# Moving the stores of x's first Fourier stage to GpSimd's queue, and cutting the last output stores another way

## The chip, the cores and the metric

The kernel runs on one core of one Trainium2 chip. The metric is the time of one execution on the device, in microseconds (us). The core has TensorE (PE, matrix products; PEld is its loading of weights), VectorE (DVE), ScalarE (ACT), GpSimd (POOL) and SyncE (SP). SP, ACT and POOL can issue DMA transfers, each in the order of its own instructions; the transfers of all three run on the same 16 DMA engines. In the profile, queue q1 is SP's, q10 ACT's and q0 GpSimd's, whose transfers are described by software on that engine.

## The reference

`u` has 2048 tokens of 448 channels. A layer norm, then the sum of the input, a state-space convolution over the tokens and a gated unit:

```python
def _A_ref(u, log_A_real, A_imag, C_real, C_imag, log_dt, D_skip):
    dt = jnp.exp(log_dt)
    A = -jnp.exp(log_A_real) + 1j * A_imag            # 448 x 256
    C = (C_real + 1j * C_imag) * dt[:, None]
    P = jnp.exp((A * dt[:, None])[:, :, None] * pos[None, None, :])
    K = 2.0 * jnp.einsum("dn,dnl->dl", C, P).real     # 448 x 2048
    y = irfft(rfft(u_t, 2 * L) * rfft(K, 2 * L), 2 * L)[:, :, :L]
    return y + u * D_skip                             # y back in token order

def _B_ref(x, w_gate, w_up, w_down):                  # 448 -> 1792 -> 448
    h = sigmoid(x @ w_gate) * (x @ w_up)
    return h @ w_down

xn = layernorm(u)
return u + _A_ref(xn, ...) + _B_ref(xn, ...)
```

## The kernel before, in words

Tokens stand in 16 blocks of 128 partitions. Two Python generators are interleaved: `glu()` is the gated unit, `conv()` the convolution. They write the program in one order, and the framework then orders each engine's instructions by a simulated timeline of its own (`schedule_with_timeline_sim=True`), within their dependences and a few explicit `issue_after` and priority marks. So an edit of one issue can move other rows.

`glu()` goes over the tokens in two halves of 8 blocks, and in each half over five groups of weight columns. For a group it makes the gate and up products (L709, tile `gu`), on ACT `th` (L717) and `hh` (L725), on DVE `hf` (L720) and `hl` (L727), then the down products (L825, tile `po`), which DVE adds to `acc` (L830). Numbers are carried as a high and a low part (`hh`, `hl`; `dh`, `dl`; `xh`, `xl`); `dl` is made on POOL (L786).

`conv()` first prepares coefficients and, for blocks 0 to 7, takes the first stage of x's Fourier transform: `x_spec` multiplies two normed blocks with a small table (L280), ACT copies the products into one of three buffers `x1a`, `x1b`, `x1c` (L293, L295) and stores them to `x1_d` in HBM, four stores for each pair of blocks. It is called four times, between 43 and 73 us. Then `kgen` makes the filter K in 56 chunks: POOL builds `me` and `mf` for two chunks at a time by repeated products (L508, L520; two buffers each), ACT squares part of `me` (L533) and makes the sines and cosines `S` (L548 to L551), DVE multiplies them into `Et` and `Ft` (L602 to L604), and PE sums over them (L616, tile `ko`).

At the end of the first half, still during `kgen`, blocks 8 to 15 are normed and transposed (`pair_norm`, `pair_turn`; L213, with the copies L219, L222, L225 on ACT and their low parts L220, L223, L226 on DVE), and `pair_first` takes their first Fourier stage: L280 again, four copies on ACT (L689), four stores on ACT's queue (L691). The copies land in tiles that share memory with `wraw` and `rd`, so the next pair's copies wait until the stores have landed. This happens four times, between 278 and 330 us.

After that, `spectra` multiplies the spectra and transforms back. The second half of `glu()` runs beside the rest of `kgen` and beside `spectra`. The function `out(src, b0, nb, ds, engs)` stores blocks `b0` to `b0+nb-1`, channels `ds`, as four DMAs, one for each 32 partitions, dealt to the queues `engs` in turn. `last(1, m)` adds the second half of the convolution's channels (L970) to all accumulators: `m` = 0, 2 to the blocks 0 to 7 (`ac`), `m` = 4, 6 to the blocks 8 to 15 (`accs[2]`, `accs[3]`). The variable `final` marks the last group of the second half: its t = 0 ends blocks 8 to 11, its t = 1 blocks 12 to 15.

Of the kernel before, what the change touches and what calls it, by code (L numbers as in the profile page):

```python
# [20 lines left out]
D = 448  # L21
# [18 lines left out]
H = D // 2  # L40
# [91 lines left out]
def s4d_glu_kernel(ctx, tc, io):  # L132
    nc = tc.nc
# [57 lines left out]
    def acc_tile():  # L191
        return pg.tile([128, 4, D], F32, name="acc", bufs=2)
# [37 lines left out]
    accs = [acc_tile() for _ in range(2)]  # L230

    def blocks(t, g, b0, nb):
        return t[g, :, b0 // 8, b0 // 4 % 2, b0 % 4 : b0 % 4 + nb]

    def out(src, b0, nb, ds, engs):

        for g in range(4):
            eng = engs[g % len(engs)]
            eng.dma_start(blocks(out_t, g, b0, nb)[:, :, ds], src[32 * g : 32 * g + 32, b0 % 4 : b0 % 4 + nb, ds])
# [33 lines left out]
    def row(b, g):  # L273
        return 32 * (b // 4 % 2) + 8 * g + 4 * (b // 8) + b % 4

    def x_first_stage(to, xn, g):

        s = slice(32 * g, 32 * g + 32)
        for i in range(2):
            nc.tensor.matmul(to[64 * i : 64 * i + 64], wx[s], xn[i][s], start=True, stop=True)  # L280

    def x_spec(xn, b0):

        x1s_ = []
        for _ in range(2):
            x1s_.append(slots[("x1a", "x1b", "x1c")[x1s[0] % 3]])
            x1s[0] += 1
        ps = psc[-1].tile([128, 2, 512], F32, name="tr", bufs=1)
        kk = [psc[-1].tile([128, 512], F32, name=n, bufs=1) for n in ("ko", "kp")]
        with tc.issue_after(glu_mm[0].ins):  # L290
            for j in range(4):
                x_first_stage((ps[:, j] if j < 2 else kk[j - 2])[:, :D], xn, j)
        nc.scalar.copy(x1s_[0], ps[:, :, :D])  # L293
        for j in range(2):
            nc.scalar.copy(x1s_[1][:, j], kk[j][:, :D])  # L295
        for p in range(2):
            r = row(b0, 2 * p)
            for h in range(2):
                to = x1_d[h].rearrange("(g r) k d -> g r k d", r=8)[r // 8 : r // 8 + 2, r % 8 : r % 8 + 2]
                nc.scalar.dma_start(to.rearrange("g i k d -> (i k) g d"), x1s_[p][:, :, H * h : H * h + H])  # L300
        yield 2 * WX

    def exp(ex, ki, fr, pl):
# [377 lines left out]
    def pair_first(b, xns):  # L681

        x1 = pg.tile([128, 2, D], F32, name="x1", tag="wraw", bufs=1)
        pss = [psg.tile([128, 512], F32, name="gu", bufs=4) for _ in range(4)]
        for g in range(4):
            x_first_stage(pss[g][:, :D], xns, g)
        for g in range(4):
            to = x1[:, g] if g < 2 else pg.tile([128, D], F32, name="x1", tag="rd", bufs=RB)
            nc.scalar.copy(to, pss[g][:, :D])  # L689
            r = row(b, g)  # L690
            nc.scalar.dma_start(  # L691
                x1_d[:, r : r + 2].rearrange("h i k d -> (i k) h d"), to.rearrange("p (h d) -> p h d", h=2)
            )

# [35 lines left out]
    def glu():  # L730
        for half in range(2):
# [4 lines left out]
            for fs_ in ORDER[half]:  # L736
# [3 lines left out]
                final = half == 1 and fs_ is ORDER[1][-1]  # L740
# [4 lines left out]
                if cross:  # L745
                    xts = {b: pair_load(b) for b in range(8, 16, 2)}
                    step = lambda f_, b: f_(b, xts[b])
                    mid = [(pair_norm, 8), None, (pair_first, 8), (pair_first, 10)]
                    end = [(), ((pair_turn, 8), (pair_norm, 10)), ((pair_turn, 10), (pair_norm, 12)), ((pair_turn, 12), (pair_norm, 14))]
                    downs = {(0, 0): (pair_first, 12), (0, 1): (pair_turn, 14), (0, 3): (pair_first, 14)}  # L750
# [54 lines left out]
                for t in range(2):  # L805
                    acc = accs[2 * half + t]
                    for b in range(4):
                        if final and (t, b) == (0, 1):

                            yield None  # L810
                        if final and t == 1 and b >= 2:

                            sp_mm[:] = glu_mm
                            for m in (4 * b - 8, 4 * b - 6):
                                lasts[0](1, m)
                            if b == 3:
                                out(accs[2], 8, 4, slice(H, D), (nc.sync, nc.scalar))
                                out(accs[3], 12, 3, slice(0, D), (nc.sync, nc.scalar))
                        po = psg.tile([128, D], F32, name="po", tag="gu", bufs=4)
                        bs = slice(128 * b, 128 * b + 128)  # L820
                        n = 0
                        with tc.issue_after(sp_mm[0].ins) if glu_on else nullcontext():
                            for (hh, hl), (dh, dl) in zip(hs[t], wts):
                                for a_, w_ in ((hh, dh), (hh, dl), (hl, dh)):
                                    glu_mm[:] = [nc.tensor.matmul(  # L825
                                        po, a_[:, bs], w_, start=(n == 0), stop=(n == 3 * fc - 1)
                                    )]
                                    n += 1
                        with hp(HP):
                            v.scalar_tensor_tensor(  # L830
                                acc[:, b], po, 0.5, acc[:, b], ALU.mult, ALU.add
                            )
                        yield 0.6 * fc
                        if cross and (t, b) in downs:
                            step(*downs[t, b])
                    if cross:
                        nc.sync.dma_start(acc_d[:, 4 * t : 4 * t + 4], acc)
                    if final and t == 0:
                        out(acc, 8, 4, slice(0, H), (nc.gpsimd,))
                    elif final:  # L840
                        out(acc, 15, 1, slice(0, D), (nc.sync, nc.scalar))

    def spectra(pf):

# [173 lines left out]
    def conv():  # L1018
        with tc.tile_pool(name="psk", bufs=1, space=PSUM) as ps_, tc.tile_pool(
# [9 lines left out]
            with tc.tile_pool(name="pst", bufs=1, side="right", reuse_waits="tile") as pst:  # L1029
# [54 lines left out]
                while preps:  # L1084
                    for p in list(preps):
                        try:
                            with tc.issue_after(hfs[max(0, len(hfs) - LAG)].ins):
                                next(p)
                        except StopIteration:
                            preps.remove(p)  # L1090
                    yield WP
                    n += 1
                    if n in (2, 3):
                        if n == 2:
                            slots["x1c"] = pst.tile([128, 2, D], F32, name="x1c", tag="raw1")
                        for b in range(0, 4, 2):
                            yield from x_spec([xns[n - 2][:, b + i] for i in range(2)], 4 * (n - 2) + b)
# [12 lines left out]
    xq, psc, raws, acl, marks, slots, pqs = list(x_first), [], [], [], [None, None], {}, []  # L1110
    W1s, GGs, act, exps = [], [], [], []
    gens = [conv(), glu()]
    total = [sum(Y0) + 11 * WP + 8 * WX + 34 + NCK * WK + HOLE + 17 * WS, 2 * (4 + NFT * 14.8) - HELD]
    done = [0.0, 0.0]
    done[0] += next(gens[0])
    held = False
    while any(g is not None for g in gens):
# [3 lines left out]
        i = min(live, key=lambda i: done[i] / total[i])  # L1121
# [33 lines left out]
```

## Time and profile before

| | us |
|---|---|
| three runs | 711.12, 714.69, 714.64 (median 714.64) |
| the profiled execution's own time | 710.54 |
| its span, first to last instruction | 708.8 |
| PE busy | 668.1 (94%) |
| DVE busy | 555.7 (78%) |
| ACT busy | 428.7 (60%) |
| POOL busy | 384.9 (54%) |

A busy time is the sum of an engine's instructions; issues of DMAs count on POOL and not on SP and ACT. A row of the timeline gives the start, how long, the engine (ACTq and SPq are the issuing side), the line, the operation and out<-in; in brackets stands the idle time before it and what ended it. A row of waits gives who waited for whom: us in sum, times, the longest. In the windows each engine has its busy time with the number of instructions.

### The profile page before, as it was taken

To read this page: it belongs to the slowest core of one execution; us is meant where nothing else is said; L and a number is where in the kernel's file an instruction comes from. 1 tells how busy PE (TensorE), PEld (TensorE's weight loads), DVE (VectorE), ACT (ScalarE), POOL (GpSimd) and SP (SyncE) were. 2 spreads that over 40 slices of the span, in tenths; PEclk is the share of its full clock that TensorE was granted. 3 is DMA by queue.
4 is the path that set the end of the run, shared out by engine and by line. 5 is a ranking of instruction groups with operands and counts; after the bars stand their busy time and mean duration, and the time that the engine had idled before them with its cause. 6 is when DMAs were issued, how large, how long until landed. Compare 5 with 4: busy or idle time off the path is not lost. (4 is left out here: it accounts for less than half of the span.)

```text
span 708.8 us, 19098 instructions
## 1 busy us (share of the span) xinstructions
PE 668.1 (94%) x7752; PEld 523.7 (74%) x7752; DVE 555.7 (78%) x766; ACT 428.7 (60%) x678; POOL 384.9 (54%) x433
## 2 busy tenths in 40 slices
PE   2798999999999998999999999999999999999996
PEld 2575878878877875756878878877777777777784
DVE  5899987699899998898478899988946555566544
ACT  3656965578689779877577788778543322322320
POOL 2101227655999999777446698798765001344001
PEclk9999999999999998989999999999999999999999
DMA  9956274554253544546833333242269988999756
GB/s 200 239 149 204 70 230 150 170 183 132 63 169 135 169 123 135 162 146 202 258 112 103 92 112 108 68 138 82 54 179 280 257 236 238 266 272 221 182 146 182
DMA packets 93031, 117.22 MB, mean 165 GB/s; under 512 B 12240, under 2 KB 76624, under 8 KB 92944
## 3 DMA queue, kind: packets, MB, share of 16 engines
q1 hardware_dynamic: 65376, 91.75, 46.3%
q10 hardware_dynamic: 24896, 18.13, 8.7%
q0 software_dynamic: 2672, 6.13, 3.2%
q8 instruction: 61, 1.00, 0.6%
q14 instruction: 26, 0.21, 0.1%
HBM read 72.13 MB, written 43.84 MB: 164 GB/s over the span
## 5 line engine op out<-in xcount | busy, mean ns | idle before, releaser
L520 POOL TENSOR_TENSOR me<-me,pm 128x32 f32<-128x32 f32 (+1 forms) x168 | 154.9, 922 | 66.8 <-DVE Et L603 38.1
L520 POOL TENSOR_TENSOR mf<-mf,pm 128x64 f32<-128x64 f32 (+1 forms) x112 | 116.9, 1044 | 5.1
L709 PE MATMUL gu<-xh,wh 128*128 128x512 f32 x336 | 100.1, 405 | 3.8 <-DVE acc L830 1.6
L709 PE MATMUL gu<-xh,wl 128*128 128x512 f32 x336 | 96.9, 393 | 0.0
L709 PE MATMUL gu<-xl,wh 128*128 128x512 f32 x336 | 95.1, 390 | 0.0
L602 DVE TENSOR_TENSOR Et<-me,S 128x1024 f32<-128x1024 f32 x56 | 80.2, 1433 | 11.6 <-ACT S L551 10.3
L825 PE MATMUL po<-dh,hh 128*128 128x448 f32 x224 | 84.2, 376 | 3.1 <-ACT hh L725 1.9
L548 ACT ACTIVATE S<-tr 128x1024 f32<-128x1024 f32 x56 | 57.7, 1030 | 44.9 <-PE tr L542 41.0
L604 DVE TENSOR_TENSOR Ft<-mf,S 128x1024 f32<-128x1024 f32 x56 | 80.1, 1431 | 5.3 <-PE ko L616 3.7
L603 DVE TENSOR_TENSOR Et<-me,S 128x1024 f32<-128x1024 f32 x56 | 80.4, 1436 | 4.8 <-ACT me L533 4.5
L825 PE MATMUL po<-dh,hl 128*128 128x448 f32 x224 | 82.4, 369 | 0.3 <-DVE hl L727 0.3
L825 PE MATMUL po<-dl,hh 128*128 128x448 f32 x224 | 82.3, 368 | 0.0
L709 PEld LDWEIGHTS gu<-xh,wh 128*128 128x128 f32 x336 | 60.8, 189 | 24.2 <-issue 4.4
L709 PEld LDWEIGHTS gu<-xh,wl 128*128 128x128 f32 x336 | 63.4, 189 | 14.7 <-DVE ve L255 0.7
L709 PEld LDWEIGHTS gu<-xl,wh 128*128 128x128 f32 x336 | 63.0, 188 | 13.5
L725 ACT CAST hh<-hf 128x512 fp32r<-128x512 f32 x56 | 34.9, 623 | 62.4 <-DVE hf L720 61.4
L616 PEld LDWEIGHTS ko<-Et,Ft 128*32 128x32 f32 x3584 | 54.7, 112 | 24.2 <-issue 13.4
L720 DVE SCALAR_TENSOR_TENSOR hf<-th,gu 128x512 f32<-128x512 f32 x56 | 38.1, 680 | 39.9 <-PE gu L709 35.2
L786 POOL TENSOR_TENSOR dl<-rd,dh 128x448 fp32r<-128x448 f32 x14 | 25.6, 1830 | 78.8 <-ACT dh L785 68.5
L616 PE MATMUL ko<-Et,Ft 128*32 128x64 f32 x3584 | 65.2, 223 | 2.6 <-DVE Ft L604 2.4
L551 ACT ACTIVATE S<-S,hpi 128x1024 f32<-128x1024 f32 x56 | 65.5, 1170 | 0.0
L717 ACT ACTIVATE th<-gu 128x512 f32<-128x512 f32 x56 | 33.5, 599 | 49.4 <-PE gu L709 43.0
(208 smaller groups left out, 1318.0 us busy)
## 6 DMA issues: line engine op xcount, KB each, us to landing
sk_d<-sk ACTq DMA_DIRECT2D x14, 512.0 KB
sx<-x_d SPq DMA_DIRECT2D x32, 224.0 KB
skl<-sk_d SPq DMA_DIRECT2D x16, 448.0 KB
vp<-v_d SPq DMA_DIRECT2D x16, 448.0 KB
v_d<-vt SPq DMA_DIRECT2D x14, 448.0 KB
ph<-ph_d SPq DMA_DIRECT2D x224, 24.0 KB
wt_d<-wh SPq DMA_DIRECT2D x9, 512.0 KB
wt_d<-wl SPq DMA_DIRECT2D x9, 512.0 KB
```

What stands on the lines that cost most here:

```text
L520: ins = nc.gpsimd.tensor_tensor(m[:, :, w + a : 2 * w : n], m[:, :, a:w:n], par(base + i).unsqueeze(2).to_broadcast([128, 4 * DC, w // n]) ...
L548: nc.scalar.activation(rows(cs), pv, AF.Abs)
L551: sins[:] = [nc.scalar.activation(cs, cs, AF.Sin, scale=-TWO_PI, bias=hpi)]
L602: v.tensor_tensor(Et[:, :, :, 32:64], two(me[:, :, 32:64]), S[:, 1::-1], ALU.mult)
L603: v.tensor_tensor(Et[:, :, :, 0:32], two(me[:, :, 0:32]), S[:, 1:3, :, ::-1], ALU.mult)
L604: fts[:] = [v.tensor_tensor(Ft, two(mf), S[:, 3:5], ALU.mult)]
L616: mm = nc.tensor.matmul(ko[32 * j : 32 * j + 32, sl], Ft[:, cc, DC * h + 4 * q + j], Et[:, cc, DC * h + 4 * q + j], start=(k == 0), stop=( ...
L709: glu_mm[:] = [nc.tensor.matmul(ps, a_, b_, start=(n == 0), stop=(n == len(mm) - 1))]
L717: marks[0] = nc.scalar.activation(th, pgu[0], AF.Tanh, scale=0.5)
L720: marks[1] = v.scalar_tensor_tensor(hf, th, 1.0, pgu[1], ALU.add, ALU.mult)
L725: nc.scalar.copy(hh, hf)
L825: glu_mm[:] = [nc.tensor.matmul(po, a_[:, bs], w_, start=(n == 0), stop=(n == 3 * fc - 1))]
```

## The change

The stores of `x_spec` and `pair_first` are issued from GpSimd instead of ScalarE. The stores at the end are cut another way: of blocks 12 and 13, the first half of the channels goes out from GpSimd as soon as block 13 has its last sum, the second half together with that of blocks 8 to 11; blocks 14 and 15 go out whole at the end. Before, blocks 12 to 14 went out whole with the second halves of 8 to 11, and block 15 at the end.

```diff
@@ x_spec
-                nc.scalar.dma_start(to.rearrange("g i k d -> (i k) g d"), x1s_[p][:, :, H * h : H * h + H])
+                nc.gpsimd.dma_start(to.rearrange("g i k d -> (i k) g d"), x1s_[p][:, :, H * h : H * h + H])
@@ pair_first
-            nc.scalar.dma_start(
+            nc.gpsimd.dma_start(
                 x1_d[:, r : r + 2].rearrange("h i k d -> (i k) h d"), to.rearrange("p (h d) -> p h d", h=2)
             )
@@ glu, t == 1, b == 3
                                 out(accs[2], 8, 4, slice(H, D), (nc.sync, nc.scalar))
-                                out(accs[3], 12, 3, slice(0, D), (nc.sync, nc.scalar))
+                                out(accs[3], 12, 2, slice(H, D), (nc.sync, nc.scalar))
@@ glu, after the add of a block
+                        if final and (t, b) == (1, 1):
+                            out(acc, 12, 2, slice(0, H), (nc.gpsimd,))
@@ glu, after the blocks of a t
                     if final and t == 0:
                         out(acc, 8, 4, slice(0, H), (nc.gpsimd,))
                     elif final:
-                        out(acc, 15, 1, slice(0, D), (nc.sync, nc.scalar))
+                        out(acc, 14, 2, slice(0, D), (nc.sync, nc.scalar))
```

How this moves instructions, at three places. First POOL, where `pair_first` works on blocks 10 and 11 beside `kgen`; `x_3772`, `x_3789` and `x_3792` are the copies of that pair, `me_1109` is the first tile of the next batch. Before:

```order
L520 TENSOR_TENSOR mf_1102<-mf_1102,pm_1167 128x32x4
L520 TENSOR_TENSOR mf_1102<-mf_1102,pm_1167 128x32x8
L520 TENSOR_TENSOR mf_1102<-mf_1102,pm_1167 128x32x16
L627 TENSOR_TENSOR ks<-ks,dm 128x8
L520 TENSOR_TENSOR me_1109<-me_1109,pm_1167 128x32
```

And now:

```order
L520 TENSOR_TENSOR mf_1102<-mf_1102,pm_1167 128x32x4
L520 TENSOR_TENSOR mf_1102<-mf_1102,pm_1167 128x32x8
L520 TENSOR_TENSOR mf_1102<-mf_1102,pm_1167 128x32x16
L691 DMA x_d<-x_3772 128x2x224 x2
L627 TENSOR_TENSOR ks<-ks,dm 128x8
L691 DMA x_d<-x_3789 128x2x224
L691 DMA x_d<-x_3792 128x2x224
L520 TENSOR_TENSOR me_1109<-me_1109,pm_1167 128x32
```

Four issues stand ahead of the next batch of `me`, and the first two behind the whole batch of `mf`. The other three pairs have theirs in the same manner, some between the products of one batch. On ACT the issues vanish from between the copies: before,

```order
L551 ACTIVATE S_1103<-S_1103,hpi 128x2x512
L689 COPY x_3789<-gu 128x448
L689 COPY x_3792<-gu 128x448
L691 DMA x_d<-x_3789 128x2x224
L691 DMA x_d<-x_3792 128x2x224
L219 CAST xh<-gu 128x2x256
```

and now the same rows without the two stores:

```order
L551 ACTIVATE S_1103<-S_1103,hpi 128x2x512
L689 COPY x_3789<-gu 128x448
L689 COPY x_3792<-gu 128x448
L219 CAST xh<-gu 128x2x256
L548 ACTIVATE S_1107<-tr 128x2x2x256
```

So the cast L219, which PE's transposes feed, stands right behind the copies. In `x_spec` the sixteen stores leave ACT likewise, and on POOL two of them come between the second and third `dl`.

Second PE, at the last pair (blocks 14 and 15). Before:

```order
L542 MATMUL tr<-sel,ph_1111 128x512 x2
L280 MATMUL gu<-xt,wx 64x448 x6
L616 MATMUL ko<-Et_1104,Ft 32x64 x11
L280 MATMUL gu<-xt,wx 64x448 x2
L616 MATMUL ko<-Et_1104,Ft 32x64 x12
L213 MATMUL gu<-ident,xt 64x128 x2
L616 MATMUL ko<-Et_1104,Ft 32x64 x7
```

Now:

```order
L542 MATMUL tr<-sel,ph_1111 128x512 x2
L280 MATMUL gu<-xt,wx 64x448 x6
L213 MATMUL gu<-ident,xt 64x128 x2
L280 MATMUL gu<-xt,wx 64x448 x2
L616 MATMUL ko<-Et_1104,Ft 32x64 x28
```

The `ko` products that stood between the stage's products now come behind them; outside this stretch and a few rows after it, PE's order is as before.

Third the end of SP's queue (ACT's has the same rows). Before:

```order
L951 DMA vp<-v_d 16x32x224
L239 DMA out_dram<-ac 32x4x224 x4
L239 DMA out_dram<-acc 32x4x224 x2
L239 DMA out_dram<-acc 32x1344 x2
L239 DMA out_dram<-acc 32x448 x2
```

Now:

```order
L953 DMA vp<-v_d 16x32x224
L239 DMA out_dram<-ac 32x4x224 x4
L239 DMA out_dram<-acc 32x2x224 x2
L239 DMA out_dram<-acc 32x4x224 x2
L239 DMA out_dram<-acc 32x896 x2
```

The second halves of blocks 12 and 13 (2 x 224) come ahead of those of blocks 8 to 11 (4 x 224), and blocks 14 and 15 (896) last. POOL's program ends with four more stores (32x2x224), behind the four of blocks 8 to 11.

## The prediction

> **What bounds the kernel now.** I read the page's busy times first, then the chain of waits, then windows by stage, then who waits for whom in the stages the change touches.
>
> ```profile
> span 708.8 us, 19098 instructions
> PE 668.1 (94%) x7752; PEld 523.7 (74%) x7752; DVE 555.7 (78%) x766; ACT 428.7 (60%) x678; POOL 384.9 (54%) x433
> PE 25%; DMA 1%; POOL 1%; issue 0%; DVE 0%; POOLq 0%
> 702.12 0.62 DVE acc L830
> ```
>
> TensorE (PE) is busy 94% of the span, and the chain that ended last is nearly all PE, up to one last add on VectorE (DVE) that ends at 702.12 + 0.62 = 702.74. What follows is stores alone. So time can be won in two ways: less PE idling, or a shorter end behind 702.74. The next rows (stretch, then us, busy time of PE, PEld, DVE, ACT, POOL, the granted clock, the DMA engines' share and GB/s) are the stages that matter: both stages that store x1, and the end.
>
> ```profile
> 40.00:76.00 36.00, 32.61 (x192) 24.30 (x191) 35.44 (x73) 23.65 (x49) 2.44 (x2) 1.00 0.60 179
> 278.00:332.00 54.00, 51.31 (x709) 32.87 (x713) 47.33 (x55) 44.12 (x74) 40.55 (x48) 0.87 0.50 158
> 272.50:279.30 6.80, 4.80 (x82) 2.08 (x81) 6.80 (x10) 6.34 (x12) 6.49 (x7) 1.00 0.11 28
> 279.30:286.10 6.80, 6.80 (x76) 4.11 (x76) 4.53 (x4) 6.80 (x14) 6.64 (x10) 0.50 0.52 165
> 310.00:316.80 6.80, 6.80 (x60) 3.97 (x63) 6.72 (x8) 5.64 (x10) 4.75 (x5) 0.50 0.31 94
> 697.40:701.10 3.70, 3.70 (x74) 2.80 (x74) 2.85 (x7) 0.00 (x0) 0.00 (x0) 1.00 0.70 183
> 702.80:707.00 4.20, 0.00 (x0) 0.00 (x0) 0.00 (x0) 0.00 (x0) 0.00 (x0) 0.88 0.93 287
> ```
>
> In the first x1 stage DVE has 35.44 of 36 us, so DVE sets its pace. In the second, PE, DVE, ScalarE (ACT) and GpSimd (POOL) are all dense, and the granted clock is 0.87, because it is 0.50 in two stretches of 6.8 us. Each such stretch costs 6.8 x 0.5 = 3.4 us of PE work. That explains the scatter of the times: the profiled execution took 710.54 and the three runs 711.12, 714.69 and 714.64; 714.64 - 711.12 = 3.5 us is one more such stretch. I take the two states to be two and three stretches. This is an inference, since only one execution has a trace.
>
> The Trainium skill (TensorE: Matmul & The Clock Gate, Part 1: The HAM clock gate) says the gate judges free-running windows of about 3.4 us and halves the clock after an idle one. The trace agrees with the half rate and with lengths of twice that, and it differs on idleness: in the 6.8 us ahead of the first stretch PE was busy for 4.80.
>
> **The x1 stores leave ACT.** 32 stores move, 16 in each x1 stage. What they cost on ACT now (duration of an issue in ns, min/median/max), and what PE waits for between 272 and 335 us:
>
> ```profile
> L300 ACTq DMA_DIRECT2D x_d<-x1ab x12: 366/409/1520, 43.2 to 72.5; - x12
> L691 ACTq DMA_DIRECT2D x_d<-x x16: 366/375/2307, 278.3 to 329.6; - x16
> 304.79 0.58 ACT L219 CAST xh<-gu 128x512 fp32r<-128x512 f32 x1 [2.41 <-issue]
> PE gu L280 <- DVE hf L720: 1.7, 2, 0.9
> PE gu L213 <- DVE xl L223: 1.5, 2, 0.8
> PE gu L280 <- DVE xl L220: 1.3, 1, 1.3
> PE gu L709 <- DVE acc L830: 0.7, 1, 0.7
> PE ko L616 <- DVE Ft L604: 0.2, 1, 0.2
> ```
>
> ACT is rid of about 32 x 0.4 = 13 us of issuing, most of it under the instruction that ACT is running anyway; one issue held it 2.41 us. But PE's waits of that stage, 5.4 us in sum, all end with DVE, none with ACT. So the gain lies between 0 and 5.4 us, and I take 0: DVE is busy 47.33 of 54 us there, and its work is not touched. A queue that is taken off an engine on which nobody waits gives nothing. The first stage has the same answer, with DVE at 35.44 of 36.
>
> **The same stores on POOL.** No x1 store has been issued there. Its price is bounded by a store of 4 x 32 = 128 runs and a load of 3 x 128 = 384 runs (after the bar: busy us and mean ns of one); behind them stand one such load by itself and, last number, the median us from issue to landing:
>
> ```profile
> L239 POOL DMA_DIRECT2D out_dram<-acc x4 | 2.2, 552 | 46.5 <-DVE acc L830 46.5
> L640 POOL DMA_DIRECT2D wraw<-in_B_w_gate_dram x5 | 3.9, 788 | 3.9 <-DMA acc<-in_A_u_dram 2.7 <-POOL dl L794 1.2
> 332.09 0.84 POOL L640 DMA_DIRECT2D wraw<-in_B_w_gate_dram  x1 [2.71 <-DMA acc<-in_A_u_dram]
> out_dram<-acc POOLq DMA_DIRECT2D x4, 112.0 KB, 2.6
> wraw<-in_B_w_up_dram POOLq DMA_DIRECT2D x5, 192.0 KB, 6.9
> ```
>
> An x1 store has 2 x 128 = 256 runs, halfway: (552 + 788)/2 = 0.67 us. Sixteen are 10.7 us on POOL in each stage. In the first, POOL is busy 2.44 of 36 us, so they fit. The one thing queued behind them is a low half `dl` (L786):
>
> ```profile
> 52.62 0.52 ACT L295 COPY x1ab<-kp 128x448 f32<-128x448 f32 x1
> 54.69 2.23 POOL L786 TENSOR_TENSOR dl<-rd,dh 128x448 fp32r<-128x448 f32 x1 [17.09 <-ACT dh L785]
> ```
>
> The two stores just ahead of it wait for the copy that ACT ends at 53.14, 1.55 us earlier, and two issues are 1.34 us, so `dl` is late by 0 if POOL issues them at once and by 1.34 if it is held until then. I take 0.
>
> In the second stage POOL has 54 - 40.55 = 13.45 us free, and 10.7 of it goes. The stores stand between the products that make `me` and `mf`, which DVE multiplies into Et and Ft, which PE waits for. How early these are ready hides the rest:
>
> ```profile
> 292.64 6.69 POOL L520 TENSOR_TENSOR me<-me,pm 128x32 f32<-128x32 f32 x6 [3.73 <-DVE Et L603]
> 300.67 3.51 POOL L520 TENSOR_TENSOR mf<-mf,pm 128x64 f32<-128x64 f32 x4
> 305.33 4.63 POOL L520 TENSOR_TENSOR me<-me,pm 128x32 f32<-128x32 f32 x6
> 319.79 4.59 POOL L520 TENSOR_TENSOR me<-me,pm 128x32 f32<-128x32 f32 x6 [4.73 <-DVE Et L603]
> 310.76 1.32 DVE L603 TENSOR_TENSOR Et<-me,S 128x1024 f32<-128x1024 f32 x1
> 312.01 1.43 DVE L604 TENSOR_TENSOR Ft<-mf,S 128x1024 f32<-128x1024 f32 x1
> ```
>
> The batch made from 292.64 is done at 299.33 (`me`) and 304.18 (`mf`) and first read at 310.76 and 312.01: a lead of 11.4 and 7.8 us. POOL then idles 4.73 us before 319.79, because its buffer is still being read. Four stores per pair are 2.7 us, less than either, so they cost DVE nothing. What is late next is ACT, which squares part of `me` in its own order, and the x1 copies of the following pair, which wait until the store before has landed. POOL's issues landed 2.6 us (stores of the end) to 6.9 us (loads) later, and the batches above are 13 to 14 us apart. I take 0 for the stage, with ends of -5.4 (all PE waits gone) and +3.4 (one more half-clock stretch).
>
> **The end.** Now, each queue (SP's and ACT's) issues six stores from 701.12 on, and its last two begin at 703.81 or earlier:
>
> ```profile
> 701.12 4.48 SPq L239 DMA_DIRECT2D out_dram<-acc  x6
> 703.81 1.79 SPq L239 DMA_DIRECT2D out_dram<-acc  x2
> out_dram<-acc SPq DMA_DIRECT2D x2, 168.0 KB
> out_dram<-acc SPq DMA_DIRECT2D x2, 56.0 KB
> 694.75 0.62 DVE L830 SCALAR_TENSOR_TENSOR acc<-po,acc 128x448 f32<-128x448 f32 x1 [1.23 <-PE po L825]
> 699.41 2.21 DVE L970 TENSOR_TENSOR acc<-acc,pv 128x448 f32<-128x448 f32 x4 [0.34 <-PE pv L962]
> ```
>
> The DMA engines are 93% busy from 702.80 to 707.00, at 287 GB/s: the end is bytes. The change takes the first half of the channels of blocks 12 and 13 out of it: 4 x 56 KB = 0.229 MB. GpSimd stores them once the add at 694.75 is done (695.37), in four issues of about 0.5 us, and they travel in the stretch 697.4 to 701.1, whose DMA share is only 0.70: room for 0.3 x 3.7 = 1.1 us of transfer, and they need 0.229/0.287 = 0.8 us. So the end becomes 0.8 us shorter. The other half of these blocks is complete after the second of four adds (699.41 + 1.1 = 700.5), 0.6 us before the first store of this group now, and the number of issues per queue stays six. Bounds: blocks 14 and 15 (0.459 MB) now all wait for the last add at 702.74, where before only block 15 did; if the engines run dry ahead of it, the doubled remainder costs 0.8 us more instead. If nothing but these bytes is left then, they are through at 702.74 + 0.3 for an issue + 0.459/0.287 = 704.6 instead of 707.0, a gain of 2.4. I take -0.8, since a share of 0.93 means no drought.
>
> **Sum.** ACT 0, POOL 0, end -0.8. Against the profiled execution that is 710.54 - 0.8 = 709.7 (its span is 708.8, with 1.7 around it); against the runs' median 714.64, 713.8. Both are the same kernel in its two states, and I can't tell which the median of the changed kernel will catch, so I forecast 712.0 for this case, with a range of its own of 709.5 to 714.
>
> **Rivals.**
> First, the second stage packs PE more densely and a half-clock stretch goes. For it: the 2.41 us hold on ACT at 302.4, right before the stretch that starts at 310.0, and the small shifts of PE's order there. Against it: no PE wait ends with ACT. It gives 709.7 - 3.4 = 706.3.
>
> Second, slower: POOL becomes the bound in the second stage because DVE stretches its issues. Its products are stretched already: the same six `me` products took 6.69 us at 292.64 and 4.59 at 319.79, 1.46 times. At 0.67 x 1.46 = 0.98 us sixteen stores take 15.6 us, 2.2 over the free 13.45, still inside the lead of 7.8. It decides beyond (13.45 + 7.8)/16 = 1.33 us a store, twice my price. At 1.8 us they are 28.8 - 21.25 = 7.5 us late, and the time is 712.0 + 7.5 = 719.5. Against it: the five loads at 788 ns average include the one at 332.09, which took 0.84 us. The Trainium skill speaks for it (SBUF — State Buffer, the box on the "DVE blocks DMA" trap): descriptors written by GpSimd starve under some VectorE copies, about 620 ns becoming about 3100. By that figure sixteen stores would take 49.6 us, an estimate from that page; no row here shows an issue on POOL so stretched.
>
> Third, the end gains nothing or loses 0.8, by the drought above: 711.3 in the one state, 715.4 in the other.
>
> **How the numbers follow.** Forecast 0.62, the rivals 0.16, 0.08 and 0.14. About 0.5% (3.6 us) can be told from no change, so faster means below 711.1 and slower above 718.2. The forecast falls on the fast side only in its lower state, 0.27 of 0.62; the first rival is faster whole, 0.16, though a fresh median of the kernel before may be lower too, so I give faster 0.40. Slower is the second rival, 0.09 with an allowance. The rest, 0.51, is the same. The range of 706 to 716.5 takes in the first and third rival and leaves out the second.
>
> **What would show it.** Right: the last store's bytes end about 0.8 us sooner after the last add; POOL's issues at L300 and L691 take near 0.67 us; DVE never waits for `me` or `mf` between 278 and 332; PE's waits there still end with DVE. Wrong: a wait of DVE's Et or ACT's squares for POOL; stores on POOL well over 1 us; or a count of half-clock stretches other than two or three, which moves the time by 3.4 us each whatever the stores do.

## The result and the profile after

The changed kernel took 719.61 us (median of 16 runs, 713.0 to 722.18) against 713.15 us for the kernel before (16 runs, 710.22 to 716.0): a ratio of 1.0084, 95% interval 1.0059 to 1.0109. It is about 6 us slower. The profiled execution took 720.06 us.

The top of its page, and the share of the chain that ended last by engine:

```profile
span 718.2 us, 19132 instructions
PE 673.0 (94%) x7752; PEld 527.2 (73%) x7752; DVE 559.9 (78%) x766; ACT 428.5 (60%) x678; POOL 412.5 (57%) x469
PE 68%; DVE 13%; DMA 5%; issue 4%; SPq 4%; ACT 4%; POOL 1%; ACTq 0%; DVEq 0%; POOLq 0%
```

POOL's busy time rose by 27.6 us, most of it the 36 stores that moved to it; ACT's did not fall, since its issues never counted as busy. The span grew by 9.4 us, more than the medians, because the execution of the kernel before that was profiled is one of its shorter ones (710.54 us). Matched instruction by instruction, PE's lag on the kernel before goes up and down between -0.5 and 3.8 us at 300 to 341 us. It is 1.6 us from 341 to 347, 8.3 us at 348 and 10.1 us at 355, and it stays at 9.5 to 9.9 us from 370 us to the last matmul. So nearly all of the loss in this trace is made between 347 and 356 us, behind the stage in which the prediction looked for it. Windows around that place (stretch, us, then busy time of PE, PEld, DVE, ACT, POOL, granted clock, DMA share, GB/s), of the kernel before:

```profile
344.00:370.00 26.00, 26.00 (x349) 20.75 (x348) 16.98 (x19) 17.14 (x25) 12.27 (x17) 1.00 0.60 160
```

and of the changed kernel:

```profile
344.00:370.00 26.00, 19.45 (x253) 15.54 (x253) 12.10 (x12) 9.08 (x14) 12.72 (x19) 0.87 0.63 184
350.15:353.56 3.41, 0.00 (x0) 0.00 (x0) 0.00 (x0) 0.00 (x0) 0.00 (x0) 1.00 0.55 207
353.57:360.39 6.82, 4.17 (x70) 3.52 (x71) 4.91 (x5) 4.81 (x7) 3.83 (x5) 0.50 0.95 235
360.39:363.80 3.41, 3.41 (x16) 2.82 (x15) 3.12 (x4) 0.76 (x2) 0.67 (x1) 1.00 0.54 117
```

Before, PE is busy all 26 us. Now it idles 6.55 us, for 3.41 us of them with all five engines still, and then has 4.17 us of work at half clock, which costs 0.5 x 4.17 = 2.1 us more. The sum, 8.6 us, is about the step in PE's lag (from 1.6 to 10.1 us). Who waited for whom at 335 to 370 us of the changed kernel (in all, times, longest):

```profile
DVE hl L727 <- ACT hh L725: 13.2, 3, 11.7
ACT hh L725 <- DMA acc_d<-acc: 12.6, 1, 12.6
PE ko L616 <- DVE Ft L604: 6.5, 1, 6.5
```

The chain of waits there (start, length, what):

```profile
344.40 8.80 DMA acc_d<-acc
...
353.27 0.32 ACTq L243
...
353.69 0.63 ACT hh L725
354.31 0.02 issue
354.33 0.69 DVE hl L727
355.03 1.15 DVE Ft L604
```

Read from below: PE's `ko` waits for Ft, which stands on DVE behind `hl`; `hl` waits for ACT's cast `hh`. `hh` itself has its data, but on ACT it stands behind a reload (L243) into the tile `acc`, and this waits until the old contents of `acc` have landed in `acc_d`. The cast, which began at 341.03 us before, begins at 353.69. Why `acc_d` was stored so late stands in SP's queue. Before, the wait of SP at 325 to 350 us for stores of x1, and two rows of its timeline:

```profile
SPq L977 <- DMA x_d<-x: 4.4, 1, 4.4
...
333.17 0.36 SPq L977 DMA_DIRECT2D t<-in_c_t_dram  x1
337.75 0.38 SPq L837 DMA_DIRECT2D acc_d<-acc  x1
```

After:

```profile
SPq L979 <- DMA x_d<-x: 9.6, 1, 9.6
...
341.21 0.36 SPq L979 DMA_DIRECT2D t<-in_c_t_dram  x1
344.40 0.79 SPq L839 DMA_DIRECT2D acc_d<-acc  x1
```

And after, ACT's last copy of x1, POOL's rows up to its last stores, and DVE's last adds into `acc`:

```profile
330.65 0.55 ACT L689 COPY x<-gu 128x448 f32<-128x448 f32 x1
...
331.96 1.22 POOL L508 TENSOR_TENSOR mf<-GG,pm 128x64 f32<-128x64 f32 x1
333.25 3.44 POOL L520 TENSOR_TENSOR mf<-mf,pm 128x64 f32<-128x64 f32 x3
336.63 0.75 POOL L691 DMA_DIRECT2D x_d<-x  x1
337.40 1.08 POOL L520 TENSOR_TENSOR mf<-mf,pm 128x512 f32<-128x512 f32 x1
338.40 1.47 POOL L691 DMA_DIRECT2D x_d<-x  x2
...
336.76 1.14 DVE L830 SCALAR_TENSOR_TENSOR acc<-po,acc 128x448 f32<-128x448 f32 x2
```

The load at L979 fills the table `t32`. This tile has the tag `rd` with two buffers, and its buffer is the one in which the last pair's third piece of x1 waits to be stored. All copies of x1 are done by 331.2 us, but POOL issues the last two stores at 338.40, behind its own products; SP's wait ends at 341.09, the load follows at 341.21, and `acc_d`, behind it in SP's queue, is stored 6.65 us later than before, though the last add into `acc` ended at 337.90.

A second thing came with the change: on ACT the planner put the first reload of `acc` ahead of `hh`. Rows of ACT before, and now:

```
L717 ACTIVATE th<-gu 128x512
L725 CAST hh<-hf 128x512
L243 DMA acc<-in_A_u_dram 32x1792 x4
```

```
L717 ACTIVATE th<-gu 128x512
L243 DMA acc<-in_A_u_dram 32x1792
L725 CAST hh<-hf 128x512
L243 DMA acc<-in_A_u_dram 32x1792 x3
```

Before, ACT waited for the same landing as well, but with `hh` already cast; what waited behind the reloads was the next `th`:

```profile
341.03 0.62 ACT L725 CAST hh<-hf 128x512 fp32r<-128x512 f32 x1 [1.03 <-DVE hf L720]
344.86 2.45 ACTq L243 DMA_DIRECT2D acc<-in_A_u_dram  x4
347.40 0.60 ACT L717 ACTIVATE th<-gu 128x512 f32<-128x512 f32 x1 [5.75 <-DMA acc<-in_A_u_dram]
```

### The profile page after: what moved, and what is told of

Read it like the earlier page. It is cut to its first block, busy times and chain, and to the rows that moved or that the text cites. A ratio compares the mean times of both kernels' runs of the same rounds, so it can differ in the third digit from the quotient of the medians.

```text
span 718.2 us, 19132 instructions
## 1 busy us (share of the span) xinstructions
PE 673.0 (94%) x7752; PEld 527.2 (73%) x7752; DVE 559.9 (78%) x766; ACT 428.5 (60%) x678; POOL 412.5 (57%) x469
## 4 chain that ended last, share of the span: by engine, by line
PE 68%; DVE 13%; DMA 5%; issue 4%; SPq 4%; ACT 4%; POOL 1%; ACTq 0%; DVEq 0%; POOLq 0%
PE gu L709 28%; PE po L825 14%; PE sp L904 7%; PE ko L616 6%; PE pv L931 4%; PE tr L542 4%; DVE Et L602 2%; SPq L492 2%; DVE Ft L604 2%; DVE Et L603 2%; DMA acc_d<-acc 1%; PE pv L964 1%; PE kp L566 1%; DMA ph<-ph_d 1%; DVE hl L727 1%
## 5 line engine op out<-in xcount | busy, mean ns | idle before, releaser
L520 POOL TENSOR_TENSOR me<-me,pm 128x32 f32<-128x32 f32 (+1 forms) x168 | 156.7, 933 | 60.4 <-DVE Et L603 31.6
L520 POOL TENSOR_TENSOR mf<-mf,pm 128x64 f32<-128x64 f32 (+1 forms) x112 | 113.4, 1013 | 5.0
L602 DVE TENSOR_TENSOR Et<-me,S 128x1024 f32<-128x1024 f32 x56 | 84.4, 1509 | 11.2 <-ACT S L551 8.3
L604 DVE TENSOR_TENSOR Ft<-mf,S 128x1024 f32<-128x1024 f32 x56 | 82.0, 1464 | 4.8 <-PE ko L616 3.4
L603 DVE TENSOR_TENSOR Et<-me,S 128x1024 f32<-128x1024 f32 x56 | 80.7, 1442 | 5.0 <-ACT me L533 4.2
L616 PEld LDWEIGHTS ko<-Et,Ft 128*32 128x32 f32 x3584 | 56.5, 115 | 31.9 <-DVE Ft L604 12.4
L616 PE MATMUL ko<-Et,Ft 128*32 128x64 f32 x3584 | 67.1, 228 | 11.3 <-DVE Ft L604 10.4
L727 DVE TENSOR_TENSOR hl<-hf,hh 128x512 fp32r<-128x512 f32 x56 | 45.4, 810 | 26.6 <-ACT hh L725 26.6
L830 DVE SCALAR_TENSOR_TENSOR acc<-po,acc 128x448 f32<-128x448 f32 x80 | 48.1, 616 | 17.8 <-PE po L825 17.8
```

The costliest lines, as they stand in the source:

```text
L520: ins = nc.gpsimd.tensor_tensor(m[:, :, w + a : 2 * w : n], m[:, :, a:w:n], par(base + i).unsqueeze(2).to_broadcast([128, 4 * DC, w // n]) ...
L602: v.tensor_tensor(Et[:, :, :, 32:64], two(me[:, :, 32:64]), S[:, 1::-1], ALU.mult)
L603: v.tensor_tensor(Et[:, :, :, 0:32], two(me[:, :, 0:32]), S[:, 1:3, :, ::-1], ALU.mult)
L604: fts[:] = [v.tensor_tensor(Ft, two(mf), S[:, 3:5], ALU.mult)]
L616: mm = nc.tensor.matmul(ko[32 * j : 32 * j + 32, sl], Ft[:, cc, DC * h + 4 * q + j], Et[:, cc, DC * h + 4 * q + j], start=(k == 0), stop=( ...
L727: v.tensor_tensor(hl, hf, hh, ALU.subtract)
```

## The experiments: the two links of the chain

The theory: SP is held by the x1 stores that POOL issues late (first link), and ACT's reload stands ahead of `hh` (second link). Each link was cut alone, and then both. The main rival is the prediction's own: POOL's stores push back POOL's products, and DVE and PE wait for these.

**`hh` ahead of the reloads, SP still held** (the edit is shortened).

```
     nc.scalar.copy(hh, hf)              ->  hhs[:] = [nc.scalar.copy(hh, hf)]
-    x_load(accs[3], 12, 4, [nc.scalar])     # at the start of glu's second half
+    with tc.issue_after(hhs[0].ins):        # after its first gate
+        x_load(accs[3], 12, 4, [nc.scalar])
```

> The changed kernel, with one thing in another order: on ACT the cast of hh (L725) now stands ahead of the four reloads of acc's second tile (L243) instead of behind the first of them; all other rows of all engines stand as in the changed kernel, and SP's late store of acc_d stays late. Theory (SP's queue is held by the load of t32, which waits for the last x1 stores; so acc_d is stored late; ACT waits for that with hh behind it; DVE and PE wait for hh): hh is cast near 342 instead of 353.7 us and the hole of PE at 348 to 356 us goes or shrinks, but ACT still stands until about 353 with the next tanh and squares behind the reloads, so only a part comes back: 713 to 717 us, 3 to 7 us less than the changed kernel, ratio to before 1.000 to 1.005. Rival A (POOL's stores push its own products back, and PE and DVE wait for these): the hole stays, 719 to 720 us, ratio 1.007 to 1.009. Rival B (nothing but a different count of half-clock stretches): as the changed kernel, 717 to 721 us.

Measured: 717.0 us, ratio 1.0045 (1.0019 to 1.0071). The order of the other four engines is that of the changed kernel.

Its timeline, its longest wait of DVE at 335 to 370 us, and its window:

```profile
341.94 0.62 ACT L725 CAST hh<-hf 128x512 fp32r<-128x512 f32 x1 [1.15 <-DVE hf L720]
...
343.54 0.38 SPq L842 DMA_DIRECT2D acc_d<-acc  x1
```

```profile
DVE hf L720 <- ACT th L717: 10.3, 1, 10.3
```

```profile
344.00:370.00 26.00, 22.35 (x325) 17.40 (x324) 12.20 (x13) 11.51 (x18) 14.60 (x22) 0.93 0.71 208
```

`hh` is cast at 341.94 and `acc_d` is stored as late as ever. ACT now waits behind `hh`, and the next tanh, and DVE's `hf` behind it, take the place of `hh`: PE still idles 3.65 us. It came out at the upper edge of what was expected: about 3 us come back.

**`t32` in a place of its own, the reload still ahead of `hh`.**

```
-    t32 = pg.tile([128, 3, 128], F32, name="t32", tag="rd", bufs=RB)
+    t32 = pf.tile([128, 3, 128], F32, name="t32", bufs=1)
```

> The changed kernel with the table t32 in a place of its own in the last stage's pool, so that SP's load of it waits for nothing that the x1 stores hold and stands 37 rows later in SP's queue; ACT's order (reload ahead of hh) and POOL's are as in the changed kernel. Theory: SP is free by 339 us, acc_d is stored 5 us sooner (338.5 to 340 instead of 344.4), lands near 346.5 to 348 instead of 353.2, and ACT's hh, DVE's hl and Ft and PE's ko come 5 to 7 us sooner, so that 4 to 7 us come back: 712 to 716 us, ratio 0.999 to 1.004. Rival A (POOL's products late behind the stores): 719 to 720 us, ratio 1.007 to 1.009, PE's hole at 348 to 356 as wide as in the changed kernel. Rival C (the landing of acc_d is late because of traffic, not because of its issue): it is issued sooner and lands no sooner than 351.

Measured: 713.99 us, ratio 1.0015 (0.9991 to 1.004). PE, DVE and POOL keep the order of the changed kernel, ACT too but for two rows near 330 us (the last copy of x1 and a cast); on ACT one reload still stands ahead of `hh`. All 32 x1 stores are on POOL. SP's load of `t32` now comes at 522.50.

Its timeline and its window:

```profile
337.57 0.38 SPq L839 DMA_DIRECT2D acc_d<-acc  x1
344.88 0.32 ACTq L243 DMA_DIRECT2D acc<-in_A_u_dram  x1
345.30 0.62 ACT L725 CAST hh<-hf 128x512 fp32r<-128x512 f32 x1 [5.05 <-DMA acc_d<-acc]
```

```profile
344.00:370.00 26.00, 25.47 (x347) 20.32 (x346) 17.07 (x18) 15.67 (x25) 16.02 (x19) 1.00 0.62 187
```

`acc_d` is stored 6.8 us sooner, the reload that waits for it begins 7.3 us after that issue, `hh` comes 8.4 us sooner, and PE's hole is 0.53 us. One tile's place gives back about 5 us with POOL's program untouched, so POOL's own products were not what was late. That ends the main rival.

**Both links cut.** POOL issues `t32`'s load, behind its own loads; the planner's order on ACT then has `hh` ahead of the four reloads.

```
-    nc.sync.dma_start(t32, io["c_t32"])
+    nc.gpsimd.dma_start(t32, io["c_t32"])
```

> The changed kernel with t32's load issued by POOL instead of SP (still into the slot of x1, so POOL waits for the landing of the last stores, behind its loads of wraw, about 1 to 3 us). Its order on ACT has hh ahead of the reloads as a side effect, so both links of the theory's chain are cut: hh near 342 us, acc_d stored by 340 and landed by 348. Theory: all of the hole goes, 710 to 714 us, ratio 0.996 to 1.001, lower than each of the two single cuts or equal to the better. Rival A (POOL's products late): POOL gets one more wait, 719 to 723 us.

Measured: 711.74 us, ratio 0.9972 (0.9954 to 0.9989): faster than either kernel. `acc_d` is stored at 339.13 and `hh` cast at 343.58. The reloads begin at 349.12, so the landing came later than the 348 that was expected; PE waited for none of it. Its window:

```profile
344.00:370.00 26.00, 26.00 (x396) 20.92 (x386) 16.80 (x17) 15.03 (x24) 19.75 (x29) 1.00 0.71 213
```

The four ratios make a table:

| | reload ahead of `hh` | `hh` ahead |
|---|---|---|
| SP held | 1.0084 (the change) | 1.0045 |
| SP free | 1.0015 | 0.9972 |

Freeing SP is worth 0.0069 and 0.0073 (4.9 and 5.2 us of 713.5), the order on ACT 0.0039 and 0.0043 (2.8 and 3.1 us); together 0.0112, 8.0 us. Each of the four differences can be off by about 2.5 us, by the intervals of its two ratios, so the first link is clear and the second only just; within that, the two add up. In the traces the second link shows where SP is held (spans of 718.2 and 714.2 us) and not where it is free (709.6 and 709.9), so its share there rests on the medians alone. PE's order, which the change moved at the last pair, is the same in all four, so it doesn't explain what differs between them.

## The experiments: parts of the change

**The stores of x1 alone, old end** (both `nc.gpsimd` lines, nothing else):

> Both pieces of x1's first stage store from POOL, the output stores at the end as in the kernel before. Order of PE and DVE as in the changed kernel. Theory (all of the loss is the hole that the x1 stores make near 350 us, the end gains 0.5 to 0.9 us): 719.5 to 721 us, ratio 1.007 to 1.011. Rival (the end costs a part of the loss): 715 to 718 us, ratio below 1.006.

Measured: 719.6 us, ratio 1.0085 (1.0064 to 1.0105). All of the loss is here. Its trace has the same chain (the last row is its window):

```profile
339.32 0.36 SPq L977 DMA_DIRECT2D t<-in_c_t_dram  x1
342.22 1.32 SPq L837 DMA_DIRECT2D acc_d<-acc  x1
351.24 0.62 ACT L725 CAST hh<-hf 128x512 fp32r<-128x512 f32 x1 [9.64 <-DMA acc_d<-acc]
...
344.00:370.00 26.00, 23.48 (x390) 18.64 (x389) 13.46 (x15) 11.84 (x18) 12.95 (x19) 0.93 0.64 194
```

But the hole is narrower: PE idles 2.52 us instead of 6.55, and its lag on the kernel before steps from 3.2 us at 344 to 7.4 at 355. So the hole of one trace is no measure of the loss of the median.

**The first half's stores alone** (L300 on POOL, L691 on ACT):

> Only the 16 x1 stores of the first half (x_spec, 36 to 76 us) are issued by POOL; the 16 of the second half (pair_first) stay on ACT, as does the order of PE. Theory: SP's load of t32 waits for stores of pair_first alone, so nothing of the loss comes: 711.5 to 714.5 us, ratio 0.998 to 1.002. Rival (POOL's packets of 256 short runs slow the first half, where the traces differ by 1.5 us at 38 to 60 us): 715 us or more, ratio 1.002 to 1.004.

Measured: 713.25 us, ratio 1.0002 (0.9979 to 1.0025). The stores of `x_spec` cost and bring nothing that these runs can tell (the interval is about 1.6 us either way), and the 1.5 us by which the changed kernel's trace lags at 38 to 60 us carry no weight: the lag is down to 0.5 us by 77.

**The last pair's four stores back on ACT:**

```
-    nc.gpsimd.dma_start(
+    (nc.scalar if b == 14 else nc.gpsimd).dma_start(
         x1_d[:, r : r + 2].rearrange("h i k d -> (i k) h d"), to.rearrange("p (h d) -> p h d", h=2)
```

> The changed kernel with the four x1 stores of the last pair of blocks (14 and 15) on ACT again, all others on POOL. The slot of t32 is then set free by a store that ACT issues. Its order on ACT has two of the four reloads ahead of hh. Theory: SP is not held beyond 335 us, acc_d is stored by 339 and landed by 347, hh near 345 to 347: as with t32 moved away, 712 to 716 us, ratio 0.999 to 1.004. Rival (any x1 store on POOL in the second half costs, by its 0.7 us each): 4 of 16 are gone, so 717 to 719 us, ratio 1.005 to 1.008.

Measured: 714.75 us, ratio 1.002 (1.0005 to 1.0036). Its timeline:

```profile
335.41 0.36 SPq L979 DMA_DIRECT2D t<-in_c_t_dram  x1
338.50 0.42 SPq L839 DMA_DIRECT2D acc_d<-acc  x1
346.97 0.62 ACT L725 CAST hh<-hf 128x512 fp32r<-128x512 f32 x1 [8.85 <-DMA acc_d<-acc]
```

Four of 32 stores carry most of the loss, and by the same link: SP is free at 335.41, and two of the four reloads still stand ahead of `hh`, where one did with `t32` moved away. PE still idles 2.92 us between 344 and 370 us. The planner's order differs from the changed kernel's at more places here, so this run alone would not settle it.

**The output stores alone** (x1 on ACT):

> The kernel before with the changed output stores alone (x1's stores stay on ACT). Theory (the loss is a hole of PE near 350 us that the x1 stores cause, the end gains about 0.5 us): 0.5 us less than before, between -1.5 and +0.3, so a ratio of 0.998 to 1.000. Rival (the end is dearer than its trace shows, for instance because POOL's four stores take DMA engines from the x_d and v_d transfers of the last stage): +1 us or more, ratio above 1.0015.

Measured: 712.52 us, ratio 0.9988 (0.9961 to 1.0016). The interval takes in no change, so the size of the gain at the end is read from the traces, below; the rival's +1 us lies just inside the interval, and only the trace speaks against it: from 650 us to the last matmul PE's lead on the kernel before stays at 1.1 us.

**The output stores and `t32` on POOL, x1 on ACT:**

> The x1 stores stay on ACT; changed are the output stores at the end and the queue of t32's load (POOL instead of SP). This tells what the x1 stores on POOL are worth once nothing waits for them: the kernel with all of the change and t32 on POOL took 711.74 us, ratio 0.9972. Theory (ACT freed of 32 issues is worth nothing by itself, as predicted): this one comes out the same within the intervals, 711 to 713 us, ratio 0.996 to 0.9995. Rival (the freed ACT does gain 1 us or more): 713 us or more, ratio 0.999 to 1.001.

Measured: 711.85 us, ratio 0.997 (0.9947 to 0.9994). With x1's 32 stores on POOL as well it was 0.9972. Once SP doesn't wait for them, the two engines make no difference that these runs can tell (about 2 us). Both versions beat both kernels.

## Why the prediction was wrong

**The step that failed** is "The same stores on POOL", where the second stage was taken as 0 with an upper end of +3.4. The question asked there was whether the stores make POOL's products late. The other half, how late the products make the stores, was answered only for the next pair's x1 copies, by the spacing of the batches ("What is late next is ACT ... and the x1 copies of the following pair"). After the last pair there is no following pair: the buffer goes to `t32`, whose load is SP's, with the store of `acc_d` behind it. The term measured about +6 us (the stores of x1 alone: ratio 1.0085, so 6.1 us of 713.7, between 4.6 and 7.5), where 0 stood. Cutting both links gives back more, 8.0 us, since the kernel so cut is 2.0 us faster than the kernel before. The end explains 0.4 to 1.0 us of these 2.0 (below); the rest lies within the interval, and no run shows a cause for it.

Two views of the kernel before held it: SP's row at 333.17, a load that waits in SP's queue for stores of x1, and ACT's wait of 5.8 us at 341 to 347 for the landing of `acc_d`, which cost PE nothing, `hh` having gone ahead. The order of ACT in the changed kernel showed the reload ahead of `hh`.

**POOL's price** was right. These are the stores of both stages (duration in ns, min/median/max, then first and last start), with the time of those of L691 to their landing, and then the sum over L691:

```profile
L300 POOL DMA_DIRECT2D x_d<-x1ab x12: 725/725/794, 44.8 to 73.6; - x12
L691 POOL DMA_DIRECT2D x_d<-x x16: 725/748/751, 282.3 to 339.1; - x16
...
DMA to landing us min/median/max: 2.5/2.9/5.9
```

```profile
L691 POOL DMA_DIRECT2D x_d<-x x16 | 11.8, 740 | 0.2 <-issue 0.2
```

That is 0.74 us a store instead of 0.67, and 11.8 us instead of 10.7. The lead hid them: between 278 and 341 us DVE waits 5.9 us in all, for PE and ACT, never for POOL, and PE's largest waits end with DVE still. The slower rival, POOL as the bound, is therefore false: it needed 1.33 us a store. Its 719.5 us agrees with the measured time by accident. The starving of GpSimd's descriptors that the Trainium skill tells of (SBUF — State Buffer, the box on the "DVE blocks DMA" trap) does not show in this trace: no issue of L691 took over 0.751 us with DVE busy 54.57 of 66 us in that stage:

```profile
278.00:344.00 66.00, 61.96 (x850) 40.95 (x849) 54.57 (x63) 53.51 (x88) 60.58 (x70) 0.90 0.48 149
```

The box ties the starving to one kind of VectorE instruction, and no run shows which of DVE's instructions here are of that kind.

**ACT freed of 32 issues** was worth 0, as said, within about 2 us: 0.9972 and 0.997 with and without it. One x1 copy now waited 2.9 us for a store to land, the wait that the prediction did name.

**The first stage** was 0, as said (1.0002, within 1.6 us).

**The end** was put at -0.8, and most traces say -0.4 to -1.0. From the end of the last add (its start plus 0.62) to the end of the span, the kernel before takes 708.8 - 702.74 = 6.06 us. The last add of the changed kernel, in its chain of waits:

```profile
712.01 0.62 DVE acc L830
```

With the output stores alone, and with both links cut:

```profile
701.03 0.62 DVE acc L830
```

```profile
704.01 0.62 DVE acc L830
```

The ends are 718.2 - 712.63 = 5.6, 706.9 - 701.65 = 5.25 and 709.9 - 704.63 = 5.3 us. With the old end it is 6.0 in the traces of x1's stores alone and of the first half's stores alone. With the new end it is 5.0 to 5.3 in three more traces (`hh` first, `t32` in a place of its own, `t32` on POOL with x1 on ACT), but 6.1 with the last pair back on ACT: no gain there, and why isn't known. The gain is short of the 2.4 us that bytes alone would allow, and in the changed kernel's last stretch the DMA engines do run dry, which was the third rival's reason but not its result:

```profile
712.70:717.00 4.30, 0.00 (x0) 0.00 (x0) 0.00 (x0) 0.00 (x0) 0.00 (x0) 0.81 0.73 229
```

Their share in the last stretch is 0.73, where it was 0.93.

**The scatter of the times** was put down to two or three half-clock stretches, and that inference doesn't hold. The 35 runs of the kernel before beside the first four experiments fill 708.51 to 715.81 us with no gap wider than 0.92 us. Their time does go with the mean granted clock (correlation -0.67), so the clock is a part of the scatter, but not in steps of one stretch. Between kernels even that fails: the profiled run with the last pair on ACT has 13.6 us at half clock ahead of the end and a span of 713.5, that with the output stores alone 17.1 us and 706.9.

**Open:** three of the changed kernel's sixteen runs took 713.0 to 714.9 us, the rest 717.8 to 722.2. What spared those three isn't known; only one run has a trace, and clock and time don't go together over the sixteen (-0.23).

## What to carry to other kernels

When a store is moved to another queue, its buffer is released later: find the next tile that gets this buffer, the queue that loads it, and every instruction behind that load, at the last turn of a loop above all, where the next owner is something else. A load that may wait belongs behind the stores that others wait for, or in a buffer of its own: one tile's place was worth 5 us here. And when the order of an engine changes at a place that no edit touches, read it: a reload ahead of a cast was worth about 3 us with SP held.

## What the runs showed of the hardware

The hole in PE's work was paid more than once. PE stood still at 350.15 to 353.56 us and was granted half clock from 353.57 to 360.39, so that 6.55 us of idling brought 2.1 us on top. This idle stretch agrees with what the Trainium skill says of the gate (TensorE: Matmul & The Clock Gate, Part 1: The HAM clock gate), unlike the half-clock stretches shown ahead of the prediction's sum, which followed work.

Such stretches are the rule here. Cut the ten traces from 26 to 700 us into pieces of 3.41 us, in step with the half-clock stretches. Half clock begins 39 times, always behind a piece in which PE was busy for 2.71 us or less, and only once behind one without any work (the hole above). All 18 pieces with less than 1.6 us of work were followed by half clock; between 1.68 and 2.71 us it came behind 21 of 91. What decides there isn't shown.

The store of `acc_d`, 896 KB in one issue, took 8.80 us from its issue to the wait that it ended in the changed kernel. Issued early, it took 7.1 us in the kernel before (337.75 to 344.86), 7.3 us with `t32` in a place of its own and 10.0 us with `t32` on POOL (339.13 to 349.12). As long as its issue was early PE waited little or not at all for it; in the changed kernel all of the 8.80 us stand in the chain of waits.
